# Fewer spare products, a re-dealt start and earlier double pieces in a recurrent-attention-and-mixture kernel

## The chip, the cores and the metric

The kernel runs on one core of one Trainium2 chip. The metric is the device time of one execution in microseconds (us). Three runs of the kernel before gave 1142.85, 1146.27 and 1148.96 us; their median, 1146.27 us, is the time to compare with. One more execution was profiled.

## The reference

Two blocks run one after the other, all in 32-bit floats.

The first is a recurrence for 4 batches x 8 heads over 768 tokens, with a state of 40x40 per head:

```python
for t in range(S):
    y[:, :, t] = np.einsum('bhd,bhde->bhe', rt, state)
    Sa = np.einsum('bhde,bhe->bhd', state, at)
    state_decay = state * wt[:, :, None, :] - np.einsum('bhd,bhe->bhde', Sa, bt)
    state = state_decay + np.einsum('bhd,bhe->bhde', vt, kt)
```

Its output, heads side by side, is x with 3072 rows (tokens) of 320. The second block is a mixture of four experts, each with a hidden width of 1024:

```python
for e in range(E):
    h = np.maximum(x @ w1[e], 0.0)
    out += p[:, e:e + 1] * (h @ w2[e])
```

where p are the given probabilities, divided by their sum.

## The kernel before, in words

**Units.** The recurrence is done in chunks of 64 tokens. A unit is one chunk of two batches, so that there are 24 units (`NU`), numbered so that units 2c and 2c+1 hold the four batches of chunk c. Inside a unit the recurrence is turned into matrix products and a triangular solve. Four generators emit its work part by part:

- `within(q)` (L384) prepares what doesn't depend on the state: decays G by a scan on VectorE (L393 to L405), the reciprocal `gp` (L412 to L414), the scaled n and k (L449 to L454), A transposed and scaled (`AT`, L456 to L459), the turned copies `NT`, `KT` (L467), the scores `pc` (L443) and the quadrants `pf` and `pe` (L477 to L485), the latter masked into `ET` and multiplied into `EV`.
- `substitute(q, eng)` (L511) solves the triangular part column by column, result `Z`. Units 0 and 1 do it on VectorE, all later ones on GpSimd (POOL).
- `merge(q)` (L563) turns `Z` into `Qc` and `QTc` (two transposes on VectorE), then does the products `pY` and `pQ`, result `QT`.
- `step(q, xT)` (L603) carries the state: `prn`, `psat`/`pst`, `pxr`, `pdy`, the new state and the output `Y`, then `Y` into its place in `xT`. For the first two chunks (`placed`, L607) that is done by six products `pxT`; from chunk 2 on by twelve DMAs per unit on SyncE's queue (L711).

**Mixture.** `xT` holds one chunk transposed: 256 columns of four batches. Units 0 and 1 get their mixture one by one (`mixture_of_unit`, 128 tokens), later chunks by `mixture_of_chunk`, 256 tokens at a time, with a seven-product scheme for the second matrix (sums of hidden values on VectorE at L835, sums of weights at L812). The mixture is cut into pieces: an `ups` piece (L718: `ph` = relu input, reads `xT`) and a `down` piece. All pieces go into one list, `todo`, in order, and `mix(n)` emits the next n of them. For a chunk the order is: up 0 of expert 0, a down piece left from the chunk before, up 1, the other down piece left over, then the same for experts 1 to 3. So a chunk's list begins with an `ups` piece of that chunk.

**The loop.** For unit u the loop emits the rest of step u, part of merge u+1, and `within` and `substitute` of unit u+2, with four gaps in between: `gap(0)` to `gap(3)`. A gap emits one piece where its number 4u+n is in `sparse`, two otherwise. `mixture_of_chunk` for chunk c is put into the list in the odd unit u = 2c+1, right after `run(s)`, which emits the last part of step u (`Y` into `xT`), and ahead of `gap(1)`.

**What sets the order.** The order on each engine is not just the order of emission: a scheduler re-arranges instructions by its own estimate of readiness, except those pinned by `keep_in_program_order`. Each engine works through its list in order. Tiles in PSUM come from two tags: `big` (5 buffers, products of the units) and `mm` (3 buffers, mixture).

**The start.** Units 0 to 2 are emitted by hand (L939 to L1014). Between the work of units 0 and 1 stand `keep_warm(n)` calls (L933): products of the identity with itself that nothing reads.

The lines that the change touches: the choice of banks for `pe` (L481), the second `keep_warm` and the hand-written start around it (L971 to L989), `sparse` and `sums_at` (L1016 to L1019), the order of the last `within` part and the first `step` part in the loop (L1035), and the place of merge's first part (L1059 to L1061).

Of the kernel before, what the change touches and what calls it, by code (L numbers as in the profile page):

```python
# [15 lines left out]
def kernel(  # L16
# [154 lines left out]
    def begin(u):  # L171
        q = Unit()
        q.u, q.c, q.bp = u, u // (B // 2), u % (B // 2)
        q.b = [2 * q.bp, 2 * q.bp + 1]
        q.start, q.end = q.c == 0, q.c == NC - 1
        q.n = {}
        units.append(q)
        return q
# [9 lines left out]
    def load_raw(q, names):  # L188


        moves = []
        for x in names:
            q.n["raw" + x] = t = raw[x]()
            heads = srcs[x].rearrange("b h t e -> (b h) t e")[q.b[0] * H:(q.b[1] + 1) * H, q.c * L:(q.c + 1) * L, :]
            heads = heads.rearrange("n (x two) e -> x n (two e)", two=2)
            for r in range(2):
                if x in "RV":

                    sets = ((slice(0, 8, 2), slice(r, 16, 4)), (slice(1, 8, 2), slice(3 - r, 16, 4)))
                else:  # L200
                    sets = ((slice(0, 8), slice(r, 16, 2)),)
                for n, hs in sets:
                    for y, w_ in enumerate((D + Q, 2 * D - Q)):
                        o = slice(64 * r + Q * y, 64 * r + Q * y + Q)
                        moves.append(lambda eng, out=t[o, n, 0:w_], in_=heads[:, hs, Q * y:Q * y + w_]: eng.dma_start(out=out, in_=in_))
        return moves
# [10 lines left out]
    def go(moves, eng=None):  # L217
        for move in moves:
            move(eng or nc.sync)
# [43 lines left out]
    def load_piece():  # L263

        k = len(pieces)
        e, x = k // 2 % E, k % 2
        if k in in_sums:
            t = sums[in_sums[k]]
        else:
            t = sb.tile([P, PIECE], FP32, name="w1p", tag="w1p", bufs=2)  # L270
        q = Piece()
        q.main = t[:, 0:2 * HF * P].rearrange("p (g c) -> p g c", g=2)
        q.last = t[:, 2 * HF * P:PIECE].rearrange("p (f c) -> p f c", c=P)
        cols = slice(x * HF * P, (x + 1) * HF * P)
        moves = [(q.main, moe_w1[e, 0:2 * P, cols].rearrange("(g p) c -> p g c", p=P))]
        for i in range(2):
            half_cols = slice((2 * x + i) * HF // 2 * P, (2 * x + i + 1) * HF // 2 * P)
            moves.append(
                (q.last[i * DT:(i + 1) * DT], moe_w1[e, 2 * P:DM, half_cols].rearrange("d (f c) -> d f c", c=P))
            )  # L280
        for to, src in moves:
            tc.keep_in_program_order(nc.sync.dma_start(out=to, in_=src))
        pieces.append(q)
# [14 lines left out]
    def load_w2(e):  # L298
        tc.keep_in_program_order(nc.sync.dma_start(out=w2_sb[e][:], in_=moe_w2[e].rearrange("(f p) d -> p f d", p=P)))
# [62 lines left out]
    def banks(name):  # L362
        return [big(f"{name}{x}") for x in range(2)]
# [20 lines left out]
    def within(q):  # L384

        n = q.n
# [91 lines left out]
        pf = quadrants(p, 0, BY_TOKENS, L, lambda j, s, i: (  # L478
            s, i ^ s, j, of_slots(q.AT, s, j, i), of_pairs(NT, s, j, i),
        ))  # L480
        if q.u == 0:  # L481
            p = banks("pe")
        pe = quadrants(p, NJ * L, BY_TOKENS, L, lambda j, s, i: (
            s, i, j, of_pairs(KT, s, j, i), of_slots(q.AT, s, j, i),
# [78 lines left out]
    def merge(q):  # L563


        Qc = sb.tile([P, H, Q], FP32, name="Qc", tag="q", bufs=2)
        QTc = sb.tile([P, H, Q], FP32, name="QTc", tag="q", bufs=2)
        tc.keep_in_program_order(nc.vector.transpose(out=dealt(Qc[:]), in_=q.Z))
        tc.keep_in_program_order(
            nc.vector.transpose(  # L570
                out=QTc[:].rearrange("p h r -> p (h r)"), in_=Qc[:].rearrange("p h c -> p (h c)"),
            )
        )
        q.QT = QTs()
        for i in range(P // Q):
            ins = nc.gpsimd.tensor_copy(out=q.QT[quarter(i), :, quarter(i % 2)], in_=QTc[quarter(i)])  # L576
            tc.keep_in_program_order(ins)
        yield

        py = big("pY")  # L580
        for h in range(H):
            for i in (1, 3):
                nc.tensor.matmul(  # L583
                    out=py[quarter(i - 1), h * Q:(h + 1) * Q], lhsT=q.F[quarter(i), h, 0:Q],
                    rhs=QTc[quarter(i), h, :], start=True, stop=True,
                )
        Y = sb.tile([P, H, Q], FP32, name="Yq")
        for i in (0, 2):
            nc.scalar.copy(out=Y[quarter(i)].rearrange("p h t -> p (h t)"), in_=py[quarter(i), 0:H * Q])
        yield  # L590

        pq = big("pQ")
        for h in range(H):
            for i in (0, 2):
                nc.tensor.matmul(  # L595
                    out=pq[quarter(i), h * Q:(h + 1) * Q], lhsT=Qc[quarter(i), h, :],
                    rhs=Y[quarter(i), h, :], start=True, stop=True,
                )
        for i in (0, 2):
            nc.scalar.copy(out=q.QT[quarter(i), :, quarter(1)], in_=by(pq[quarter(i), 0:H * Q], Q))  # L600
        yield
# [301 lines left out]
    def begin_later(n):  # L903
        for move in later[:n]:
            tc.keep_in_program_order(move(nc.sync))
        del later[:n]
# [8 lines left out]
    def run(gen, n=99):  # L915
        if gen is None:
            return
        for _ in range(n):
            if next(gen, gen) is gen:
                break  # L920
# [3 lines left out]
    def begin_step(u):  # L924
        q = units[u]
        if q.bp == 0:
            chunks_x[q.c] = sb.tile([P, 3, 2 * P], FP32, name="xT", tag="xT", bufs=2)
        q.xT = chunks_x[q.c][:, :, q.bp * P:(q.bp + 1) * P]
        return step(q, q.xT)
# [3 lines left out]
    def keep_warm(n):  # L933

        for _ in range(n):
            ins = nc.tensor.matmul(out=warm[:, 0:P], lhsT=ident[:], rhs=ident[:], start=True, stop=True)
            tc.keep_in_program_order(ins)

    ws = [within(units[u]) for u in range(3)]  # L939
# [23 lines left out]
    m, s = merge(units[0]), begin_step(0)  # L963
# [6 lines left out]
    load_piece()  # L970
    run(ws[1], 1)  # L971
    run(norm, 1)
    keep_warm(18)
    run(ws[1], 1)
    run(m)
    run(ws[2], 1)
    run(norm)
    load(units[2], "BK")
    go(load_raw(units[2], "A"))
    go(load_raw(begin(3), "W"))  # L980
    load_w2(0)
    load_piece()
    load_piece()
    load_w2(1)
    load_piece()
    run(s, 2)
    run(ws[1], 1)
    run(s)
    run(ws[1], 2)  # L989

# [8 lines left out]
    m, s = merge(units[1]), begin_step(1)  # L999
# [13 lines left out]
    run(ws[3], 1)  # L1013
    mix(1)  # L1014

    sparse = range(4 * 1, 4 * 4 + 2)  # L1016

    sums_at = {4 * 2 + n: 1 for n in range(1, 11)}
    sums_at.update({4 * 4 + 3: 2, 4 * 5 + 0: 3, 4 * 5 + 1: 2, 4 * 5 + 2: 3})  # L1019
    sum_ops = (None for e in range(E) for _ in add_weights(e))  # L1020
    for u in range(1, NU):
        q = units[u]
        m = s_next = w = w_next = iter(())
        if u + 1 < NU:
            m, s_next = merge(units[u + 1]), begin_step(u + 1)
            w_next = ws[u + 1]
        if u + 2 < NU:
            w = ws[u + 2]

        def gap(n, pieces=None):  # L1030
            at = 4 * u + n
            run(sum_ops, sums_at.get(at, 0))
            mix((1 if at in sparse else 2) if pieces is None else pieces)

        run(w_next)  # L1035
        run(s, 1)
        gap(0)


        early = u < 5  # L1040
        if early:
            run(s, 1)
        run(w, 1)
        run(s)
        if u == 1:
            mixture_of_unit(q)
        elif q.bp:
            mixture_of_chunk(units[u - 1:u + 1], chunks_x[q.c])
        begin_later(len(later))
        run(w, 1)  # L1050
        if not early:
            run(m, 1)
        gap(1)

        if u + 3 < NU:
            go(load_raw(begin(u + 3), "WA"))
            load(units[u + 3], "WBKV")
            later.extend(load_raw(units[u + 3], "VR"))
        run(w, 2)  # L1059
        if early:  # L1060
            run(m, 1)  # L1061
        else:
            run(s_next, 1)
            run(m, 1)
        gap(2)

        if not early:
            run(m, 1)
        run(w, 1)
        if not early:  # L1070
            run(s_next, 1)
        if u + 2 < NU:
            substitute(units[u + 2], nc.gpsimd)
        run(w, 1)
        if u + 3 < NU:
            ws.append(within(units[u + 3]))
            run(ws[u + 3], 1)
        if early:
            run(m, 1)
            run(s_next, 1)  # L1080
            run(m)
            gap(3, 1)
            run(s_next, 1)
            mix(0 if 4 * u + 3 in sparse else 1)
        else:
            gap(3)
        s = s_next
# [31 lines left out]
```

## Time and profile before

| | |
|---|---|
| median of 3 runs | 1146.27 us (1142.85 to 1148.96) |
| time of the profiled execution | 1141.15 us |
| its span, first to last instruction | 1139.1 us |
| TensorE (PE) busy | 1099.4 us, 97% |
| VectorE (DVE) busy | 757.8 us, 67% |
| GpSimd (POOL) busy | 473.6 us, 42% |
| ScalarE (ACT) busy | 338.0 us, 30% |
| mean granted TensorE clock | 0.988 |
| DMA queue 1 (from SyncE) | 119.12 MB, 42.7% of 16 engines |

PE is the matmul side of TensorE, PEld its weight loads, a q behind an engine's name its instruction queue, so that SPq is SyncE issuing DMAs. In timelines the columns are the start in us from the span's start, the duration in us, engine, line, operation, output<-inputs, shapes, and how many instructions were merged into the row; a pair in square brackets is idle time ahead of the row and what ended it. In tables by stretch each engine has its busy time and its number of instructions, then come the granted clock of TensorE (1.00 is full), the share of the DMA engines and GB/s. Every number below about one execution is from the profiled one; the median of the runs is 5.1 us above it.

### The profile page before, as it was taken

The numbers are of one execution on the slowest core, as the hardware profiler recorded it, in microseconds if no ns is written. First come the engines' busy times: TensorE is split into PE (matmuls) and PEld (weight loads), VectorE is DVE, ScalarE is ACT, GpSimd is POOL, SyncE is SP. The second block draws the span as 40 slices with busy tenths as digits, with TensorE's granted clock in tenths as the row PEclk, the third lists the DMA queues.
The fourth block names the chain that finished last, engine by engine and source line by source line (L and its number), as shares of the span: only waits on it lengthen the run. The fifth ranks groups of instructions, "written<-read, shape, count | busy, mean of one in ns | idle before, by whom it ended". The sixth has DMA issues, their size and how long they took to land.

```text
span 1139.1 us, 38245 instructions
## 1 busy us (share of the span) xinstructions
PE 1099.4 (97%) x16036; PEld 976.6 (86%) x16036; DVE 757.8 (67%) x1553; ACT 338.0 (30%) x860; POOL 473.6 (42%) x1221
## 2 busy tenths in 40 slices
PE   6899997999999999999999999999999999999998
PEld 5777776888998989889899898888989898888887
DVE  8756647697767768667677677677677586553343
ACT  2333333333233232332332332332332322311110
POOL 4005626662724635625526526437337246340000
PEclk8899998999999999999999999999999999999999
DMA  7784643254263454444453453443543442231330
GB/s 118 213 245 124 131 99 78 65 132 101 76 146 89 107 128 100 119 122 101 115 121 83 123 118 86 118 102 84 139 102 87 117 110 64 75 90 55 105 92 12
DMA packets 268867, 122.16 MB, mean 107 GB/s; under 512 B 213737, under 2 KB 242073, under 8 KB 268697
## 3 DMA queue, kind: packets, MB, share of 16 engines
q1 hardware_dynamic: 265416, 119.12, 42.7%
q8 instruction: 126, 2.06, 0.8%
q10 hardware_dynamic: 3280, 0.61, 0.3%
q14 instruction: 45, 0.36, 0.1%
HBM read 111.79 MB, written 3.93 MB: 102 GB/s over the span
## 4 chain that ended last, share of the span: by engine, by line
PE 87%; DVE 4%; SPq 2%; DMA 2%; POOL 2%; ACT 2%; issue 1%; DVEq 0%; ACTq 0%
PE ph L734 29%; PE p L841 28%; PE ph L726 9%; PE pdy L371 4%; PE pfe L371 2%; PE psat L371 2%; PE pxr L371 2%; PE prn L371 2%; PE po L775 2%; PE pQ L595 1%; PE pc L371 1%; PE pY L583 1%; PE pev L371 1%; POOL Z L557 1%; PE pg L335 1%
## 5 line engine op out<-in xcount | busy, mean ns | idle before, releaser
L734 PE MATMUL ph<-xT,w1p 128*128 128x256 f32 (+1 forms) x1520 | 344.1, 379 | 2.2 <-issue 2.2
L734 PEld LDWEIGHTS ph<-xT,w1p 128*128 128x128 f32 x1520 | 274.3, 190 | 65.1 <-issue 27.3
L544 POOL TENSOR_TENSOR Z<-M,Z 128x62 f32<-128x62 f32 (+7 forms) x352 | 143.3, 407 | 368.6 <-DVE M L535 336.0
L557 POOL TENSOR_TENSOR Z<-Z 128x31 f32<-128x31 f32 (+7 forms) x704 | 257.2, 365 | 55.2
L835 DVE TENSOR_TENSOR a<-hs 128x512 f32<-128x512 f32 x220 | 152.4, 710 | 128.2 <-ACT hs L739 128.2
L739 ACT ACTIVATE hs<-ph 128x512 f32<-128x512 f32 (+1 forms) x208 | 115.7, 564 | 295.5 <-PE ph L734 295.1
L841 PE MATMUL p<-sums,a 128*128 128x160 f32 x1056 | 165.1, 299 | 0.0
L752 DVE SCALAR_TENSOR_TENSOR osb<-p,gate,osb 128x320 f32<-128x320 f32 (+1 forms) x243 | 107.9, 481 | 74.9 <-PE p L841 70.9
L841 PEld LDWEIGHTS p<-sums,a 128*128 128x128 f32 x1056 | 152.9, 190 | 2.3
L726 PE MATMUL ph<-xT,w1p 64*128 64x256 f32 (+1 forms) x760 | 110.1, 398 | 1.2 <-issue 1.1
L841 PE MATMUL p<-w,hs 128*128 128x160 f32 x704 | 102.9, 299 | 0.0
L841 PE MATMUL p<-w,a 128*128 128x160 f32 x704 | 102.8, 299 | 0.0
L841 PEld LDWEIGHTS p<-w,hs 128*128 128x128 f32 x704 | 100.3, 190 | 2.2
L841 PEld LDWEIGHTS p<-w,a 128*128 128x128 f32 x704 | 98.0, 190 | 0.0
L576 POOL COPY QT<-QTc 32x256 f32<-32x256 f32 x96 | 51.6, 537 | 111.5 <-DVE QTc L570 103.7
L726 PEld LDWEIGHTS ph<-xT,w1p 64*128 64x128 f32 x760 | 67.8, 187 | 14.4 <-issue 4.4
L519 DVE STREAM_TRANSPOSE M<-blocks 128x1024 f32<-128x1024 f32 x24 | 47.0, 1957 | 23.1 <-ACT blocks L516 23.0
L414 DVE RECIPROCAL gp<-gp 128x320 f32<-128x320 f32 x24 | 51.7, 2152 | 0.8
L504 ACT COPY EV<-pev 64x160 f32<-64x160 f32 x96 | 23.4, 286 | 66.8 <-PE pev L371 66.3
L371 PE MATMUL pdy<-VC,k_tok 64*64 64x104 f32 (+1 forms) x768 | 41.6, 260 | 0.1
L600 ACT COPY QT<-pQ 32x256 f32<-32x256 f32 x48 | 17.4, 362 | 79.3 <-PE pQ L595 78.8
L626 ACT COPY SN<-prn 128x256 f32<-128x256 f32 x44 | 15.7, 370 | 84.1 <-DVE RH L621 81.9
(148 smaller groups left out, 1364.0 us busy)
## 6 DMA issues: line engine op xcount, KB each, us to landing
w1p<-in_moe_w_dram SPq DMA_DIRECT2D x95, 512.0 KB
w1p<-in_moe_w_dram SPq DMA_DIRECT2D x190, 64.0 KB
w<-in_moe_w_dram SPq DMA_DIRECT2D x4, 1280.0 KB
sums<-in_moe_w_dram SPq DMA_DIRECT2D x9, 512.0 KB
natW<-in_w_dram SPq DMA_DIRECT2D x48, 80.0 KB
natB<-in_b_dram SPq DMA_DIRECT2D x48, 80.0 KB
natK<-in_k_dram SPq DMA_DIRECT2D x48, 80.0 KB
out_dram<-osb SPq DMA_DIRECT2D x46, 80.0 KB
```

Of the source, the lines that this page charges most:

```text
L371: nc.tensor.matmul(out=p[row][half(col), lo + at * out_cols:lo + (at + 1) * out_cols], lhsT=lhsT, rhs=rhs, start=(n == 0), stop=(n == len( ...
L414: pin(nc.vector.reciprocal(out=gp[:], in_=gp[:]))
L519: ins = nc.vector.transpose(out=M[:], in_=cols)
L544: ins = eng.tensor_tensor(out=Z[:, 1:3, 0:n, j + 1:Q], in0=M[:, j:j + 2, None, j + 1:Q].to_broadcast([P, 2, n, m]), in1=Z[:, here, 0:n, j: ...
L557: eng.tensor_tensor(out=z[:, 0], in0=z[:, 0], in1=z[:, x], op=ALU.add)
L576: ins = nc.gpsimd.tensor_copy(out=q.QT[quarter(i), :, quarter(i % 2)], in_=QTc[quarter(i)])
L726: nc.tensor.matmul(out=ph[i][:, f, :], lhsT=w1.last[i * DT:(i + 1) * DT, f, :], rhs=xT[i * DT:(i + 1) * DT, 2, :], start=(f == 0), stop=False,
L734: nc.tensor.matmul(out=ph[i][:, f, :], lhsT=w1.main[:, g, at * P:(at + 1) * P], rhs=xT[:, g, :], start=False, stop=(g == 1 and f == HF // ...
L739: nc.scalar.activation(out=h[:, i * HF // 2:(i + 1) * HF // 2, 0:n], in_=ph[i][:], func=ACTF.Relu,)
L752: nc.vector.scalar_tensor_tensor(out=to, in0=p, scalar=sc, in1=to, op0=ALU.mult, op1=ALU.add)
L835: nc.vector.tensor_tensor(out=t[:], in0=x, in1=y, op=op)
L841: nc.tensor.matmul(out=p[:, n * HD:(n + 1) * HD], lhsT=a[:, f, :], rhs=b[:, f, :], start=(f == 0), stop=(f == HF - 1),)
```

## The change

There are seven edits, none of which changes what is computed except that sixteen products without a reader are left out.

1. `pe` gets its own pair of banks in all units that start a batch (units 0 and 1), not in unit 0 alone.
2. The second `keep_warm` goes from 18 products to 2.
3. In the start, the first parts of step 0 move ahead of the first part of `within(2)`, of the second part of `normalize` and of several DMA issues; the loads of `W` for unit 3 move behind `load_w2(0)` and two mixture pieces' weights.
4. `sparse` ends at gap 4*3+2 (exclusive) in place of 4*4+2: gaps 2 and 3 of unit 3 and gaps 0 and 1 of unit 4 emit two pieces in place of one. The extra piece at the end of unit 3 follows the same test.
5. `sums_at` deals the same twenty sums of weights over gaps that end two gaps earlier.
6. In the loop the first part of step u comes ahead of the last part of `within(u+1)`.
7. For units 1 and 2 the first part of merge moves ahead of the scores of `within(u+2)`.

```diff
-        if q.u == 0:
+        if q.start:
             p = banks("pe")
...
-    keep_warm(18)
+    keep_warm(2)
     run(ws[1], 1)
     run(m)
-    run(ws[2], 1)
+    run(s, 2)
+    run(ws[1], 1)
+    run(s, 1)
     run(norm)
     load(units[2], "BK")
     go(load_raw(units[2], "A"))
-    go(load_raw(begin(3), "W"))
     load_w2(0)
     load_piece()
     load_piece()
+    run(s, 1)
+    run(ws[2], 1)
+    go(load_raw(begin(3), "W"))
     load_w2(1)
     load_piece()
-    run(s, 2)
-    run(ws[1], 1)
     run(s)
     run(ws[1], 2)
...
-    sparse = range(4 * 1, 4 * 4 + 2)
-
-    sums_at = {4 * 2 + n: 1 for n in range(1, 11)}
-    sums_at.update({4 * 4 + 3: 2, 4 * 5 + 0: 3, 4 * 5 + 1: 2, 4 * 5 + 2: 3})
+    sparse = range(4 * 1, 4 * 3 + 2)
+
+    sums_at = {4 * 2 + n: 2 if n == 4 else 1 for n in range(1, 10)}
+    sums_at.update({4 * 4 + 2: 2, 4 * 4 + 3: 3, 4 * 5 + 0: 2, 4 * 5 + 1: 3})
...
+        run(s, 1)
         run(w_next)
-        run(s, 1)
         gap(0)
...
-        run(w, 2)
+        run(w, 1)
+        if u < 3:
+            run(m, 1)
+        run(w, 1)
         if early:
-            run(m, 1)
+            run(m, 1 if u >= 3 else 0)
```

## The prediction

> **What bounds the kernel now.** First the page's head, the busy times and the clock by slices:
>
> ```profile
> span 1139.1 us, 38245 instructions
> ...
> PE 1099.4 (97%) x16036; PEld 976.6 (86%) x16036; DVE 757.8 (67%) x1553; ACT 338.0 (30%) x860; POOL 473.6 (42%) x1221
> ...
> PE   6899997999999999999999999999999999999998
> ...
> PEclk8899998999999999999999999999999999999999
> ```
>
> TensorE is the bound, idle for 39.7 us of the span. So an edit is worth what it takes from or adds to TensorE's idle time, or to its time at a low clock. Where is the idle time? The summary of waits on TensorE:
>
> ```profile
> PE pev L371 <- DVE ET L382: 6.7, 2, 5.9
> PE pY L583 <- DVE QTc L570: 6.5, 3, 4.9
> PE psat L371 <- issue: 3.1, 3, 1.5
> ```
>
> No wait on a DMA or on `xT` stands in it. The 4.9 us lie in unit 3; the timeline and the clock there:
>
> ```profile
> 191.89 1.07 PE L583 MATMUL pY<-QTc,F 32*32 32x32 f32 x32 [4.86 <-DVE QTc L570]
> ```
>
> ```profile
> 189.00:190.00 1.00, 0.00 (x0) 0.00 (x0) 0.00 (x0) 0.00 (x0) 0.71 (x4) 0.97 0.46 69
> 190.00:191.00 1.00, 0.00 (x0) 0.00 (x0) 0.73 (x2) 0.00 (x0) 0.22 (x1) 0.50 0.82 122
> ...
> 199.00:200.00 1.00, 1.00 (x4) 0.82 (x3) 1.00 (x1) 0.00 (x0) 0.92 (x2) 0.50 0.09 22
> 200.00:201.00 1.00, 1.00 (x5) 0.81 (x5) 0.96 (x3) 0.01 (x1) 0.77 (x4) 0.91 0.00 0
> ```
>
> The idle time costs twice: 3 us after the last product (187.0) the clock halves, and it comes back 8.2 us after work resumes. From `pY` to the end of the next `ups` piece it took 191.89 to 202.61, 10.72 us; the same five groups one unit later took 230.02 to 237.07, 7.05 us. The cold clock cost 3.7 us.
>
> Last, what follows the state update of an odd unit in the steady part (unit 11, timeline of TensorE, SyncE, VectorE):
>
> ```profile
> 520.34 0.42 PE L371 MATMUL pdy<-SX,n_tok 64*64 64x104 f32 x6
> 520.69 1.13 PE L726 MATMUL ph<-xT,w1p 64*128 64x256 f32 x8
> ...
> 525.31 2.34 PE L841 MATMUL p<-w,hs 128*128 128x160 f32 x16
> ...
> 528.57 0.60 PE L335 MATMUL pNT<-ident,n_tok 128*128 128x128 f32 x4
> ```
>
> ```profile
> 524.14 9.09 SPq L711 DMA_DIRECT2D xT<-Y  x12
> ```
>
> ```profile
> 523.43 0.68 DVE L687 TENSOR_TENSOR Y<-Y,G 128x512 f32<-128x512 f32 x1
> ```
>
> `pdy` ends at 520.76 and a mixture piece follows at once. `Y` is there at 524.11 (+3.35), since the reciprocal holds VectorE; SyncE then issues twelve transfers until 533.23 (+12.5). In the trace's DMA records the last of their packets (512 B) ends at +13.3 (unit 11), +13.1 (units 15 and 21). So a chunk is complete 13.5 us after its `pdy`. Today nobody waits: the list holds four pieces of the chunk before.
>
> **What the Trainium skill says.** "TensorE: Matmul & The Clock Gate", section "What's actually happening": one idle window of about 3.4 us halves the clock, a busy one restores it. The trace agrees on the fall (3.0 us), and shows 8.2 us for the return. The same page, section "The mechanism": matmuls start and end in strict order, only weight loads are pulled ahead. So a product waiting for `xT` holds all behind it. "DMA: Bandwidth & Descriptors", section "Rules for kernel authors": issue a DMA early and wait for it late. The kernel before does so, its trace has no such wait.
>
> **The change part by part.** *Pieces per gap (edit 4).* I counted the list. Before, odd unit 5 emits at gaps 1, 2, 3: (c1 up, down), (c1 up, down), (c2 up, c1 down). With four pieces consumed earlier, the list is empty at `gap(0)` of unit 5 and every later odd unit, and `gap(1)` begins with the new chunk's first `ups` piece. No gap runs short of pieces; but the first reader of `xT` now stands right behind its making. In the built order of the changed kernel's TensorE instructions, odd units read: `pdy`, `pNT`, `pKT`, `pc`, `prn`, `pY`, some `pQ` and `pfe`, then `ph<-xT`, which waits on DMA semaphores. The scheduler moved the next unit's work into the hole; what it has for it is 528.57 to 531.72 in the rows above (`pNT` to `pY`), 3.15 us, and about 0.35 us of `pQ`/`pfe`: 3.5 us. So idle time per chunk is 13.5 - 3.5 = 10.0 us. That is also what VectorE allows: `pfe` waits for the scaled `AT`, behind Qc (POOL's `Z` at 527.96, +7.2), QTc, G, VC, scan and RH; adding their durations gives +13.0.
>
> Chunks 3 to 10: 8 x 10.0 = 80 us. Chunk 2 (unit 5) is worse: in SyncE's built order four loads of raw `A` now precede its `xT`, and they wait for VectorE's transpose of unit 7's `AT`, which stands behind `Y` (+4.9 in unit 5), states, n, k, one sum, G's scan and VC: about +11.6; 1.9 us for four issues, 8.2 for twelve, 1.6 to land: +23.5, so 20 us idle. Chunk 11 (unit 23): nothing but the piece follows `pdy`; the last packet there ended at +11.3: 11.3 us. Sum 111 us.
>
> *Cold clock.* Ten such holes, each with TensorE nearly idle for over 3 us. Bounds: 1.9 us each (half of 3.8 us, the time from the start of the spare products, 32.43, until the clock rose at about 36.2) and 3.7 us (above). I take 3.0: 30 us.
>
> *The same edit in units 3 and 4.* The extra piece in front of `pY` covers 4.86 us and keeps the clock, 3.7 us; taken from between `pQ` and `psat`, it uncovers some 2 us there (copies of QT and SaT, 0.75 and 0.65 us, with their waits). Net -6.5.
>
> *Spare products (edit 2).* QTc is done at 33.0; `pY` started at 38.49, behind 6.14 us of spare products. The window can give 5.5 us, less what the cold clock takes: these products brought the clock from 0.50 to 1.00. Without them the chain `pY` to `pxT`, some 9.6 us of TensorE, runs colder, up to 5 us longer. Gain 0 to 5.5; I take 2.
>
> *Start (edit 3).* G's scan of unit 2 (2.6 us of VectorE) moves into later idle time of VectorE (1.5 and 0.8 us around 50); what is late next is unit 1's `Z`, with 5.4 us to spare (QTc 69.4, `pY` 74.83). On SyncE the raw `W` of unit 3 (2.6 us of issue) goes behind `w2` and two weight pieces: those start earlier, and `W` isn't read before 95. Own banks for `pe` (edit 1): the `F` copies start 0.5 us earlier, `pe` waits for the two banks of `pc`; same spare time. Nothing for these; without that cover about 1 us either way. *Edits 5 and 6*: sums of 0.8 us on an engine 67% busy, and `pev` behind `pxr`, where pieces stand between anyway: nothing. *Edit 7*: QTc of unit 3 no longer waits for the scores at 159.8 (its `Z` was done at 143.5): the 0.96 us before `pY` at 161.62 and part of 1.44 us before `psat`; -1.5.
>
> Sum: 111 + 30 - 6.5 - 2 - 1.5 = +131. Profiled execution: 1139.1 + 131 = 1270 us of span, 1272 us own time; on the median, 5.1 us above that one, 1277 us.
>
> **Rivals.**
>
> *Shorter holes.* SyncE, less contended, could issue at its quickest (0.55 us in place of 0.75: 2.4 us less per chunk), or the clock returns after one busy window. 111 - 24 + 15 - 10 = +92: 1238 us. For it: the minimum of the issue durations is 554 ns. Against: twelve issues took 8.2 us or more in every unit.
>
> *Longer holes.* While TensorE stands, SyncE holds the next weights behind it, and POOL's loop (M to `Z` 24.4 us) starts later; 3.5 us more per chunk: 1312 us. Against: by my count the weights of the two pieces after the hole are issued before `xT`.
>
> *Faster.* The early gains stand alone, -10 us: 1136 us. That needs `xT` within 3.5 us of `pdy`; it decides where the hole per chunk falls under 1 us. For it: the list never runs short and TensorE's work is 5.4 us less. Against: 9 us of issue alone.
>
> *The change doesn't do what it says*: the scheduler could have put a down piece of the old chunk ahead of `ph`, which would cut each hole by 3.5 us. The built order shows that it didn't.
>
> **How the numbers follow.** Holes as worked out 0.58, its own range 1253 to 1300; shorter 0.21; longer 0.15; faster or none 0.06. The forecast is that of the first, 1277 us. The range, 1222 to 1315, leaves out the fast case and the tails. Within 0.5% (5.7 us) is about what a measurement can't tell from no change. Faster by more 0.05, within 0.02, slower 0.93.
>
> **What the profile after would show.** Right: in the waits of TensorE a new line, `ph L726` (or `L734`) on a DMA `xT<-Y` or on VectorE, ten times, 7 to 11 us each if idle time is cut by `pNT` to `pfe` into parts (`pNT <- n_tok` about 4 us, the rest in front of `pfe` and `ph`); PEclk down to 6 or 7 tenths in ten slices; PE's share at about 87%; odd units 13 us longer, even ones unchanged; no 4.9 us in front of `pY` in unit 3, and `pY` of unit 0 at about 34. Wrong: if `ph<-xT` follows `pdy` without a hole, the count of the list or the landing time is wrong; if the holes are there and the clock stays at 1.00, the 30 us go.

## The result, and the profile after

The changed kernel takes 1295.1 us (median; 1284.7 to 1302.3) against 1146.2 us for the kernel before, measured beside it: a ratio of 1.129, 95% interval 1.121 to 1.138. The forecast was 1277 us. The profiled execution took 1284.66 us with a span of 1282.8 us; it is the lowest of the times measured. The account below, by the trace, is of 143.7 us of span; some 5 us of the difference between the medians are outside it.

The page's head after the change, with TensorE's busy share and clock by slices:

```profile
span 1282.8 us, 38129 instructions
...
PE 1165.2 (91%) x16004; PEld 1024.9 (80%) x16004; DVE 754.0 (59%) x1553; ACT 344.3 (27%) x860; POOL 469.8 (37%) x1221
...
PE   6898988976998998998998998998999899799698
...
PEclk7899988997997997998998899899799799799799
```

The smooth row of nines is now notched once per chunk, in the busy row and in the clock row. TensorE is busy for 65.8 us more, with 32 instructions fewer: work at half clock takes longer, and counts as busy. The summary of waits on TensorE (us in total, times, longest):

```profile
PE pNT L335 <- DVE n_tok L450: 54.7, 11, 15.3
PE ph L726 <- DMA xT<-Y: 14.5, 4, 11.1
...
PE pQ L595 <- ACT Yq L589: 6.4, 11, 1.6
...
PE pfe L371 <- ACT SN L626: 3.8, 7, 0.5
```

`pNT` now waits ten or so times for `n_tok`, and `ph` for the transfers into `xT`. Here is one hole close up: the timeline of TensorE behind the `pdy` of unit 11, which ends at 593.73, and the clock in the same stretch (the figure before the DMA share):

```profile
598.15 1.12 PE L335 MATMUL pNT<-ident,n_tok 128*128 128x128 f32 x4 [4.42 <-DVE n_tok L450]
...
602.84 1.06 PE L583 MATMUL pY<-QTc,F 32*32 32x32 f32 x32
604.37 0.31 PE L595 MATMUL pQ<-Yq,Qc 32*32 32x32 f32 x2 [0.46 <-ACT Yq L589]
...
606.67 0.74 PE L595 MATMUL pQ<-Yq,Qc 32*32 32x32 f32 x20
607.34 2.12 PE L726 MATMUL ph<-xT,w1p 64*128 64x256 f32 x8
609.40 4.54 PE L734 MATMUL ph<-xT,w1p 128*128 128x256 f32 x16
```

```profile
595.70:597.70 2.00, 0.00 (x0) 0.00 (x0) 2.00 (x7) 0.00 (x0) 1.71 (x4) 0.94 0.75 121
597.70:599.70 2.00, 1.55 (x7) 1.39 (x8) 1.90 (x4) 0.40 (x1) 1.66 (x5) 0.50 0.08 21
...
609.70:611.70 2.00, 2.00 (x7) 1.65 (x7) 0.00 (x0) 0.00 (x0) 0.00 (x0) 0.65 0.61 112
```

`ph` starts 13.6 us after `pdy`; the chunk's last packet ends at +13.2. In six of the eight odd units from 7 on, this one among them, `pQ` ends just as `ph` begins, so that no wait for the transfers shows; whether they or the slow work in front set the start is left to the experiments. Only 5.4 us of the hole are idle; the rest is filled by `pNT` to `pQ`, stretched by the half clock (5.8 us from `pNT` to `pY`, 3.15 us in the kernel before). The clock stays down until about +17, although TensorE works again from +4.4 on.

Adding up the time from one `pdy` to the next against the kernel before (where a mixture piece has moved from one unit to another, its duration is taken out): start to unit 5 +6.1, unit 5 +23.4, the eight odd units 7 to 21 together +98.5 (12.3 each), the even units between them +1.2, the tail behind unit 23 +14.6; in all 143.8 us. So 136.5 us arise behind the `pdy` of odd units and nearly nothing anywhere else in the steady part.

### The profile page after: what moved, and what is told of

Same layout as the page of the kernel before. It is cut to its first block, busy times and chain, and to the rows that moved or that the text cites. A ratio compares the mean times of both kernels' runs of the same rounds, so it can differ in the third digit from the quotient of the medians.

```text
span 1282.8 us, 38129 instructions
## 1 busy us (share of the span) xinstructions
PE 1165.2 (91%) x16004; PEld 1024.9 (80%) x16004; DVE 754.0 (59%) x1553; ACT 344.3 (27%) x860; POOL 469.8 (37%) x1221
## 4 chain that ended last, share of the span: by engine, by line
PE 67%; DVE 11%; POOL 10%; SPq 3%; issue 3%; DMA 3%; ACT 3%; DVEq 0%; ACTq 0%; POOLq 0%
PE ph L734 24%; PE p L841 21%; PE ph L726 8%; POOL Z L557 7%; POOL Z L544 4%; SPq L711 2%; PE psat L371 2%; PE pdy L371 2%; PE pfe L371 2%; PE po L775 2%; DVE M L519 2%; PE pxr L371 1%; PE pQ L595 1%; DVE a L835 1%; DVE gp L414 1%
## 5 line engine op out<-in xcount | busy, mean ns | idle before, releaser
L734 PE MATMUL ph<-xT,w1p 128*128 128x256 f32 (+1 forms) x1520 | 357.6, 390 | 0.0
L734 PEld LDWEIGHTS ph<-xT,w1p 128*128 128x128 f32 x1520 | 284.6, 198 | 69.2 <-issue 25.8
L544 POOL TENSOR_TENSOR Z<-M,Z 128x62 f32<-128x62 f32 (+7 forms) x352 | 140.4, 399 | 527.7 <-DVE M L535 481.5
L557 POOL TENSOR_TENSOR Z<-Z 128x31 f32<-128x31 f32 (+7 forms) x704 | 254.3, 361 | 55.2
L726 PE MATMUL ph<-xT,w1p 64*128 64x256 f32 (+1 forms) x760 | 120.7, 426 | 14.9 <-DMA xT<-Y 14.5
L726 PEld LDWEIGHTS ph<-xT,w1p 64*128 64x128 f32 x760 | 74.5, 201 | 29.3 <-issue 19.8
L576 POOL COPY QT<-QTc 32x256 f32<-32x256 f32 x96 | 46.9, 489 | 103.1 <-DVE QTc L570 98.1
L335 PE MATMUL pNT<-ident,n_tok 128*128 128x128 f32 x96 | 19.5, 340 | 54.7 <-DVE n_tok L450 54.7
L335 PEld LDWEIGHTS pNT<-ident,n_tok 128*128 128x128 f32 x96 | 13.7, 170 | 57.4 <-DVE n_tok L450 52.6
L667 ACT COPY RS<-pxr 64x256 f32<-64x256 f32 x88 | 32.3, 367 | 87.9 <-DMA rawR<-in_r_dram 51.8
```

Source lines behind the costliest of these rows:

```text
L544: ins = eng.tensor_tensor(out=Z[:, 1:3, 0:n, j + 1:Q], in0=M[:, j:j + 2, None, j + 1:Q].to_broadcast([P, 2, n, m]), in1=Z[:, here, 0:n, j: ...
L557: eng.tensor_tensor(out=z[:, 0], in0=z[:, 0], in1=z[:, x], op=ALU.add)
L726: nc.tensor.matmul(out=ph[i][:, f, :], lhsT=w1.last[i * DT:(i + 1) * DT, f, :], rhs=xT[i * DT:(i + 1) * DT, 2, :], start=(f == 0), stop=False,
L734: nc.tensor.matmul(out=ph[i][:, f, :], lhsT=w1.main[:, g, at * P:(at + 1) * P], rhs=xT[:, g, :], start=False, stop=(g == 1 and f == HF // ...
```

## The experiments

The theory: four pieces of the old chunk stood between `pdy` and the first reader of the new `xT`, edit 4 spends them early, and what TensorE then lacks is bounded by the landing of `xT`. Rivals: the re-dealt start makes the loss; VectorE's chain and not `xT` ends the hole; the low clock is a price of its own. Where the spans of single units are compared, they come from one profiled execution each, and the first units differ by several us between executions of like code: the `pdy` of unit 2 ends at 140.7 us in the changed kernel and at up to 147.2 us in the runs that share its start.

### Pieces per gap alone, and all but these

Edits 4 and 5 alone on the kernel before:

```diff
-    sparse = range(4 * 1, 4 * 4 + 2)
+    sparse = range(4 * 1, 4 * 3 + 2)
```

(with `sums_at` as in the change), and the changed kernel with just that taken back.

> The kernel before with edits 4 and 5 alone (pieces per gap and sums of weights). Theory: the four pieces of the old chunk that stood between pdy and the first reader of xT are gone, and that alone makes the time: +111 of holes and +30 of cold clock, as in the changed kernel, less what units 3 and 4 may gain; 1146 + 130 to 150, so 1275 to 1297 us. Rival: the re-dealt start, own banks or the moved first part of the step cost it: then this kernel stays within 10 us of 1146.

> The changed kernel with edits 4 and 5 taken back (edits 1, 2, 3, 6 and 7 remain). By the prediction's working: -2 for the spare products and -1.5 for edit 7, so 1142.5 us. By the trace of the changed kernel (units 0 to 3): -2.3 until unit 0's pdy, then +2.9 and +4.0 in the next two units and -0.5, so about +4: 1150 us. Rival (these edits cost the 144 us): 1290.

Measured: 1279.0 us for the pieces alone (ratio 1.116, 1.112 to 1.120), 1161.8 us for all the rest (1.013, 1.010 to 1.016). So edit 4 with 5 makes 132 us of the 149, as the theory says, and the rest makes 15, which neither the prediction (-3.5) nor the first reading of the trace (+4) had. The two add up to the whole within 2 us. Edit 5 was not run apart from edit 4.

Taken unit by unit, as above, the trace of the pieces alone is less kind to the prediction: units 3 and 4 together are 6.8 us longer (forecast: 6.5 us shorter), unit 5 is 15.4 us longer (forecast: 23), the odd units 7 to 21 together 99 us and the tail 14 us. The longest wait of `psat`, 6.4 us, lies in unit 3 and is new:

```profile
PE psat L371 <- DVE RH L621: 7.9, 2, 6.4
```

The piece that stood there is gone, and four sums of hidden values, which follow the `ups` pieces brought forward (2.6 us of VectorE, from 196.12 on), stand in front of `RH`. From this wait on the clock is at half for 17.1 us.

### What stands in front of the reader: two down pieces first

```diff
+            if before and e == 0:
+                todo.extend(before)
+                todo.append(lambda e=e: ups(e, 0))
+                todo.append(lambda e=e: (ups(e, 1), add_h(e)))
+                before = [lambda e=e: down_1(e), lambda e=e: down_2(e)]
+                continue
             todo.append(lambda e=e: ups(e, 0))
```

> The changed kernel, but each chunk's list begins with the two down pieces left from the chunk before, then its two ups pieces (in place of one, one, one, one). The work is the same. Theory: what matters is only what stands between pdy and the first reader of xT. Two down pieces of some 3.5 us each, and pNT to pY (3.5 us) make 10.5 of 13.5 us; 3 us of idle time stay per chunk, too short for the clock to fall: the odd units' excess goes from 12.3 to about 3.5 us, unit 5's from 23 to 15, the tail's from 14.6 to 7; so 1295 - 85 = 1210 us. Rival: pieces of the old chunk only move the hole, since the list is short by four pieces whatever its order: 1285 to 1300.

Measured: 1223.1 us (1.067, 1.064 to 1.070), 72 us less than the changed kernel with the same work. Order alone does it; the rival falls. The gain stayed 13 us short of the 85 expected, and the reason is in the trace. TensorE behind the `pdy` of unit 7, and its clock a little later:

```profile
405.50 0.69 PE L583 MATMUL pY<-QTc,F 32*32 32x32 f32 x32
408.22 2.84 PE L726 MATMUL ph<-xT,w1p 64*128 64x256 f32 x8 [2.03 <-DMA xT<-Y]
410.99 5.60 PE L734 MATMUL ph<-xT,w1p 128*128 128x256 f32 x16
```

```profile
407.00:408.00 1.00, 0.00 (x0) 0.00 (x0) 1.00 (x4) 0.00 (x0) 0.00 (x0) 1.00 0.07 21
408.00:409.00 1.00, 0.78 (x2) 0.51 (x3) 0.96 (x3) 0.00 (x0) 0.00 (x0) 0.51 0.14 37
```

The wait is 2.03 us, as worked out, but the clock halves just as work resumes and stays low until 414.8: the `ups` piece takes 8.4 us in place of 4.86. "Too short for the clock to fall" was wrong. The odd units 7 to 21 keep 5.5 us each (12.3 in the changed kernel), not 3.5.

### When xT lands: two queues, then both together

```diff
+        queues = [nc.sync, nc.scalar]
         for h in range(0 if placed else H):
...
-                    nc.sync.dma_start(
+                    queues.reverse()
+                    queues[0].dma_start(
```

> The changed kernel with the twelve transfers of a unit's Y into xT issued in turn by SyncE and ScalarE. Theory (the landing of xT ends the hole, and its length is the issue time of twelve transfers in one queue): 6 issues in place of 12 are 4.5 us less; xT is complete at about +9 and the holes are 4.5 us shorter in ten chunks: about 1250 us. Rival (the scaled AT, at +13.0 on VectorE, ends the hole whatever xT does; or packets and not issues set the landing): within 10 us of the changed kernel, 1285 to 1300.

Measured: 1269.8 us (1.107, 1.103 to 1.110): 25 us less, between the two expectations. The packets do land at +9.0 to +9.4 as worked out, but the first `ph` starts at +10.2 and TensorE waits for no transfer in the steady units: 4.4 us for `n_tok`, then part of `pNT` to `prn` at half clock, ahead of `ph` in the queue. So the landing no longer ends the hole; the next term does. The sharper test removes both terms:

> The changed kernel with the two left-over down pieces first in each chunk's list, and xT issued by two queues. Theory: work without need of xT stands behind pdy until +10.9 (7 us of down pieces, pNT to pY; measured with the down pieces first), and xT is complete at +9.0 (measured with two queues): no hole is left in the odd units from 7 on and in the tail, so from 1223 us nine times some 5 us of hole and cold clock go: 1175 to 1185 us, of which 1162 are what the kernel without the new pieces per gap takes and the rest is unit 5. Rival (something else than the reader of xT makes the odd units long): 1205 us or more.

Measured: 1182.2 us (1.034, 1.031 to 1.036), inside the expected span. TensorE's waits and clock:

```profile
PE p L843 <- DVE w L814: 13.6, 2, 12.0
PE ph L728 <- ACT hs L741: 8.3, 8, 1.2
...
PEclk8798799898999999999999999999999999999999
```

No wait for `xT` or `n_tok` is left in the odd units from 7 on, and the clock row stands at nine from there. They keep 2.1 us each (the clock still fell for 3.4 us in units 9 and 11), 1.2 of it where a second `ups` piece directly behind the first waits for ScalarE to empty its banks. The 12.0 us are unit 5, below. That closes the main question for these units and the tail: what the change costs there is the distance from `pdy` to the landing of `xT`, minus the work at hand to fill it, and the low clock that follows.

### Is the low clock a price of its own?

Spare products, which nobody reads, in front of the first `ups` piece of each chunk from chunk 2 on:

```diff
-            todo.append(lambda e=e: ups(e, 0))
+            if e == 0 and qs[0].c >= 2:
+                todo.append(lambda e=e: (fill(24), ups(e, 0)))
+            else:
+                todo.append(lambda e=e: ups(e, 0))
```

> The changed kernel with 24 spare products (identity with itself, about 3 us, nobody reads them) in front of each chunk's first ups piece from chunk 2 on, so that TensorE has something to do right behind pdy. pNT to pY then run at full clock (3.15 us in place of the 5.8 us measured in the changed kernel). Theory: xT lands at +13.5 and ends the hole, so what runs slowly inside it costs nothing; only cold work behind the landing counts, and the clock, falling later, is still low there: 1295, within 12 us. Rival (the cold clock inside the hole is part of its price): 2.65 us less in each of nine holes and a little behind them, 1265 to 1271 us.

Measured: 1303.1 us (1.139, 1.137 to 1.141): no gain. TensorE behind the `pdy` of unit 11 (ends at 601.10):

```profile
601.03 5.62 PE L909 MATMUL fill<-ident 128*128 128x128 f32 x48
606.49 0.60 PE L335 MATMUL pNT<-ident,n_tok 128*128 128x128 f32 x4
...
613.91 2.85 PE L726 MATMUL ph<-xT,w1p 64*128 64x256 f32 x8 [3.67 <-issue]
616.70 5.34 PE L734 MATMUL ph<-xT,w1p 128*128 128x256 f32 x16
```

`pNT` to `pY` run at full clock, and TensorE just waits longer; `ph` starts at +12.8. The clock falls during that wait and the first piece of the chunk pays (8.2 us from 613.91 on, 6.7 us in the changed kernel). My price for a spare product was half of what it is (0.234 us, two instructions of 0.117), so `pNT` was 1.0 us late. The test is less clean for that, but the rival's 24 to 30 us are nowhere. The bracket names no releaser, but the chunk's last packet ends at +13.2 here as well, and with the work in front done at +9.1 the transfers are what is left: the slow work of the changed kernel moved `ph` by 0.8 us at most. `pfe`, which VectorE's chain feeds, comes only behind `ph` here, so that chain doesn't end the hole either.

With two queues, where slow work did seem to end the hole:

> Both changes together: xT issued by two queues (complete at +9.0 instead of +13.5, as the run with two queues showed) and the 24 spare products. Theory: with two queues alone the hole no longer ended with xT but with pNT to pY, which started at +4.4 and ran at half clock until +10.2. With both, pNT to pY end at +7.5 and xT at +9.0 ends the hole, with only 1.5 us of idle time and the clock never down: excess of an odd unit 9.0 - 3.5 = 5.5 us in place of 12.3, so about 1295 - 65 = 1230 us; the two together give more than their sum. Rival (the two effects add): the result of two queues, 1270, plus that of the spare products alone.

> The changed kernel with xT issued by two queues and 16 spare products behind pdy, in place of the 24 that took 5.6 us and so made pNT late. 16 take some 3.7 us, less than the 4.4 us that TensorE waits for n_tok. The order of TensorE is that of the run with two queues alone (1270 us). Theory: there a part of pNT to prn ran at half clock from +4.4 to +10.2 and ended the hole; at full clock it ends at about +7.2 and xT at +9.0 does: 2 to 3.5 us less in each of nine holes, 1238 to 1252 us. Rival (the clock inside the hole is worth nothing, as with one queue): 1263 to 1270 us.

Measured: 1263.6 us (1.105, 1.103 to 1.108) with 24 products and 1265.0 us (1.106, 1.103 to 1.108) with 16. Both theories missed, and the first rival too (1278 us by its sum); the second rival, no gain, held. The intervals overlap that of two queues alone. With 24 the scheduler put `ph` ahead of most of the ready work. With 16 the order stayed, and the trace shows what else is in the way; ScalarE (its queue and its copies) and then TensorE behind the `pdy` of unit 11, at 590.87:

```profile
594.28 4.41 ACTq L713 DMA_DIRECT2D xT<-Y  x6
598.73 0.59 ACT L436 COPY NT<-pNT 128x512 f32<-128x512 f32 x1 [7.41 <-DVE Qc L568]
```

```profile
599.37 0.51 PE L371 MATMUL prn<-state,AT 64*64 64x40 f32 x19 [1.66 <-ACT NT L436]
...
600.25 2.24 PE L728 MATMUL ph<-xT,w1p 64*128 64x256 f32 x8
```

The six issues hold ScalarE's queue for 4.41 us (issuing is not counted as busy, so the bracket names another engine). The copy of `NT` stands behind them, `prn` waits for the copy, and `ph` stands behind `prn`. The second queue moved the transfers off SyncE onto an engine that TensorE needed. That is not all of the missing gain: `ph` starts at +9.4 here, 0.3 us after the last packet, and the clock falls all the same, for 3.4 or 6.8 us in each odd unit from 7 to 21. How the rest divides is not shown.

### Where the other 15 us come from

Edit 7 alone, edits 1, 2, 3 and 6 alone, and edit 6 alone, each on the kernel before, as in the change's diff:

> The kernel before with edit 7 alone. Theory from the traces: in unit 1 VectorE's transposes Qc and QTc, which wait for POOL's Z, now stand ahead of the transpose RT of unit 3; RT ends at 113.6 in place of 110.7, pc waits 1.4 to 2.8 us for it, the clock falls, and unit 1 becomes 4 to 12 us longer: 1150 to 1158 us. Rival (the prediction's step: QTc of unit 3 comes earlier and nothing else is touched): 1145 us.

> The kernel before with edits 1, 2, 3 and 6 (the changed kernel without edits 4, 5 and 7). Theory (edit 7 made the 15 us that the kernel with all but the pieces lost): pdy of unit 0 2.3 us earlier, unit 0 to 1 1 to 3 us longer, nothing else: 1145 to 1149 us. Rival (own banks or the moved parts of the start make it): 1155 to 1162 us.

> The kernel before with edit 6 alone: the first part of the step (prn, RH, SN) ahead of the last part of within (pev, EV). The prediction costed it at nothing. In the kernel with edits 1, 2, 3 and 6 pNT waits 2.6 us for n_tok in unit 3 and pdy 1.5 us for VC in unit 4, which the kernel before does not show. If edit 6 makes these: 1148 to 1153 us. If the start makes them: within 3 us of the kernel before.

Measured: edit 7 1151.2 us against 1144.5 (1.0060, 1.0047 to 1.0074), so +6.6; edits 1, 2, 3 and 6 1152.9 us (1.0068, 1.0048 to 1.0089), so +8.4; edit 6 alone 1148.5 us against 1143.2 (1.0047, 1.0031 to 1.0063), so +5.3. Edit 7 and the others add up to the 15. The second result lies between its two expectations, the other two are as expected.

*Edit 7* did what was expected. Here is VectorE in unit 1, in the kernel before and then with edit 7 alone:

```profile
110.02 0.70 DVE L223 STREAM_TRANSPOSE RT<-rawR 128x512 f32<-128x512 f32 x1
...
115.57 0.62 DVE L568 STREAM_TRANSPOSE Qc<-Z 128x256 f32<-128x256 f32 x1 [2.40 <-POOL Z L557]
```

```profile
118.76 0.62 DVE L568 STREAM_TRANSPOSE Qc<-Z 128x256 f32<-128x256 f32 x1 [4.98 <-POOL Z L557]
119.41 0.45 DVE L570 STREAM_TRANSPOSE QTc<-Qc 128x256 f32<-128x256 f32 x1
119.78 0.71 DVE L223 STREAM_TRANSPOSE RT<-rawR 128x512 f32<-128x512 f32 x1
```

`Qc` waits for POOL's `Z`, and `RT`, which is ready, now stands behind it. `pc` then waits 5.2 us for `RT` (a wait of TensorE that the kernel before doesn't have) and the clock falls for 10.2 us in that unit, which is 7.7 us longer in this profile. In the changed kernel the same wait is 1.44 us.

*Edit 6* costs what was expected, and the rival falls. Here is VectorE around the end of `pdy` of unit 3 (at 174.88 before), in the kernel before and then with edit 6 alone (`pdy` ends at 183.14):

```profile
173.28 0.49 DVE L413 TENSOR_TENSOR gp<-pg,natW 128x320 f32<-128x320 f32 x1 [0.34 <-PE pg L335]
...
178.09 0.47 DVE L450 SCALAR_TENSOR_TENSOR n_tok<-natB,gp 128x320 f32<-128x320 f32 x1
```

```profile
185.31 0.47 DVE L413 TENSOR_TENSOR gp<-pg,natW 128x320 f32<-128x320 f32 x1
...
188.45 0.48 DVE L450 SCALAR_TENSOR_TENSOR n_tok<-natB,gp 128x320 f32<-128x320 f32 x1
```

In the kernel before, `gp` and its reciprocal run while TensorE still does `pdy`. With edit 6 `pg` comes on TensorE right behind `pdy`, so `gp`, the reciprocal and `n_tok` come after the state update, and `pNT` waits 2.57 us. In unit 4 `pdy` waits 2.23 us for ScalarE's copy `RS`. So edit 6 makes new waits, but how its 5.3 us come about is not shown. In the same trace the 4.86 us in front of `pY` shrink to 0.8, and unit 3 is 1.7 us shorter, not longer. The longer units are 0, 2 and 4 (by 3.9, 2.9 and 3.2 us), and in 0 and 2 the waits on TensorE are nearly those of the kernel before; what differs is the clock, at half for 6.8 us in each.

### A version that might beat both

The kernel before with edit 2, and 16 spare products, pinned in front of `pY`, that fill the 4.86 us of unit 3 and so hold the clock:

```diff
-    keep_warm(18)
+    keep_warm(2)
...
+        if u == 3:
+            fill(16, units[u + 2].F)
         if early:
             run(m, 1)
```

> The kernel before with edit 2 (2 spare products in place of 18), and with 16 spare products put where TensorE waits 4.86 us for QTc in unit 3, behind pfe, so that the clock stays up. By the traces: unit 0's pdy 2.3 us earlier, and the 3.7 us of cold clock in unit 3 saved: -6 us, a ratio of 0.995. Rival (both gains are taken back by the next wait): within 2 us of the kernel before.

Measured: 1141.9 us against 1143.2 us (0.9991, 0.9978 to 1.0004): no difference, as its rival had it. In its trace units 3 to 5 take 4.1 us less, as forecast, and the clock is full in unit 3; but unit 3 begins 4.1 us later, though unit 0's `pdy` ended 1.9 us earlier. In both kernels the `pdy` of unit 6 ends at 301.05. Whether the missing spare products cost that is open: the kernels with edit 7 or 6 alone, which keep all 18, show a like loss between units 0 and 1 in their profiles (3.3 and 3.9 us, half clock for 6.8 us).

## Why the prediction was right, and where it was not

*Pieces per gap.* The mechanism was right, and the size too in the steady units and the tail. The count of the list and the landing at +13.5 held: `ph` starts at +13.6. The terms for the holes, the clock and units 3 and 4 (111 + 30 - 6.5) make +134.5; alone on the chip, edits 4 and 5 gave +132, interval +128 to +137. That the sums agree so well is in part luck: units 3 and 4 came out 13 us worse than forecast there, unit 5 some 8 us and the odd units from 7 on some 5 us better.

*Inside the hole* the terms were nearly right in sum and wrong in kind. Per chunk the prediction had 10.0 us idle and 3.0 us of cold clock, 13.0; measured 12.3, of which 5.4 us are idle. The missing idle time is `pNT` to `pQ` at half clock, and the spare products showed that slow work inside the hole costs little (0.8 us at most in the start of `ph`). The low clock costs behind the landing: the first `ups` piece takes 6.7 us, not 4.86. For the same reason the share of TensorE was 91%, not 87%: slow work counts as busy.

*Unit 5.* The number was right by luck (`ph` expected at +23.5, found at +23.9; with the pieces alone it starts at +16.6), for its reason was wrong. The prediction had SyncE's loads of raw `A` wait for VectorE, with `xT` behind them. These are SyncE's and VectorE's rows in the changed kernel, where `pdy` ends at 280.38:

```profile
277.32 1.88 SPq L205 DMA_DIRECT2D rawA<-in_a_dram  x4
294.77 8.88 SPq L711 DMA_DIRECT2D xT<-Y  x12
```

```profile
283.63 0.61 DVE L568 STREAM_TRANSPOSE Qc<-Z 128x256 f32<-128x256 f32 x1 [10.79 <-POOL Z L557]
...
294.07 0.68 DVE L687 TENSOR_TENSOR Y<-Y,G 128x512 f32<-128x512 f32 x1
295.14 0.47 DVE L450 SCALAR_TENSOR_TENSOR n_tok<-natB,gp 128x320 f32<-128x320 f32 x1
```

The loads were issued before `pdy` ended. VectorE stood 10.8 us in front of `Qc`, waiting for POOL's `Z`, with sums of hidden values, `Y` and `n_tok` behind it. It is of the kind of edit 7: a transpose that waits for POOL, ahead of ready work. With the down pieces first and two queues the hole stays (12.0 us), since these pieces wait for weight sums on the same VectorE.

*Tail.* Right: 11.3 us were forecast and 11.1 us waited; with the clock 14.3 us were forecast and 14.6 us measured.

*Units 3 and 4, -6.5.* Failed. The 4.86 us in front of `pY` are gone, as forecast. But the step that took the piece from in front of `psat` was mis-sized: some 2 us were to be uncovered there, and with the pieces alone it is 6.4 us, with the clock at half for 17.1 us behind it; +6.8 us in all. In the changed kernel there are 2.5 us in front of `psat` and 2.6 us in front of `pNT` (edit 6), the clock is at half for 13.7 us, and the two units are some 2 us longer.

*Edits 6 and 7.* Failed, and this is where most of the 18 us between forecast and median lie. Edit 7 was costed by what it lets start earlier in unit 3 (-1.5); it also applies to unit 1, where it moves a waiting transpose ahead of `RT`: +6.6. Edit 6 was costed at nothing because pieces stand between its two halves; it moved `pg` behind `pdy` and made new waits, and alone it costs 5.3 us, of which the trace explains only a part. In both, the order of VectorE was not followed past the instruction that moved.

*Edits 1, 2 and 3.* Unit 0's `pdy` ends 2.3 us earlier, as forecast; behind it the own banks of `pe` wait 1.07 us for those of `pc`, which was foreseen. The clock falls before the next `pdy` too, but 43 us later, behind another wait (1.2 us of `pev` for `ET`). Beside edit 6 (5.3 of 8.4) they cost about 3 us, within the noise of both runs.

*Rivals.* The rival of shorter holes fell: twelve issues take 8.85 us or more in all ten odd units from 5 on. That of longer holes fell too: the holes of the steady part weren't longer, and the distance above 1277 us is mostly edits 6 and 7. That of a faster kernel fell.

## What to carry to other kernels

A queue of ready work in front of the first reader of a slow transfer is worth the distance it covers; count it in time at the reader, and before spending it early ask what will stand there instead. When a step that waits on another engine is moved forward in an in-order queue, walk down that queue and price everything ready behind it, in every iteration that the edit touches. When one term of a wait is shortened, work out the next term first: two queues halved the issue time and gained 25 us of the 45 expected.

## What the runs showed of the hardware beyond expectation

An idle stretch of 2.03 us was enough to halve TensorE's clock, from the moment work resumed and for 6.8 us: half of that, 3.4 us, comes on top of the wait itself. The Trainium skill, "TensorE: Matmul & The Clock Gate", section "What's actually happening", puts the fall after at least one idle window of about 3.4 us; in seven of the eight odd units with the down pieces first, waits of 2.0 to 2.8 us at `ph`, and in two of these units one more of 1 to 2 us, went with time at half clock, so here the measurement decides. In front of the wait of 2.03 us stand 3.2 us of small products, `pNT` to `pY`. Without a wait, in the kernel before, they leave the clock up; whether they count in part as idle time when a wait follows is not shown. What agrees is the grain: worked out from the mean granted clock, the time at half clock between two `pdy` came out near 3.4, 6.8, 10.2, 13.7 or 17.1 us in nearly all of the steady units, multiples of one window.

Twelve small transfers from one queue take 8.9 us to issue and six from ScalarE 4.41 us, about 0.74 us each on either engine. The copy behind the six on ScalarE starts at 598.73, just when the last of them is issued (598.69).
